# A new first third of the order table of an attention and MLP-mixer kernel

## The chip, the cores and the metric

The kernel runs on one core of a Trainium2 chip. The metric is the device time of one execution in microseconds (us). One core has a matrix engine (TensorE, in the profile PE; its weight loads are listed as PEld), a vector engine (DVE), a scalar engine (ACT), GpSimd (POOL) and SyncE (SP), each with an instruction stream of its own that is worked off in order, and DMA engines that move data between the device memory and the core's on-chip memory. Engines wait for one another and for loads through semaphores.

## The reference

Eight batches, 8 heads, 576 positions, head width 64. Attention is causal in blocks of 64 positions. Its output, with the heads side by side (512 columns), goes through a mixer: two matrices over the positions, then two over the columns, each pair with a relu between and a residual.

```python
scores = (q @ k.T) / sqrt(64)                 # per batch and head, 576 x 576
scores = where(pos_i // 64 >= pos_j // 64, scores, -1e9)
x = softmax(scores) @ v                       # -> x: 8 x 576 x 512
u = x + (relu(x.T @ w_tok1) @ w_tok2).T       # w_tok1 576 x 256, w_tok2 256 x 576
out = u + relu(u @ w_ch1) @ w_ch2             # w_ch1 512 x 1536, w_ch2 1536 x 512
```

Inputs and output are float32. The kernel computes its matrix products in bfloat16.

## The kernel before

The program first describes its work as 1,591 small operations, each with the engines that it may run on, the operations that it depends on, and the matrix result banks (PSUM banks) that it takes and gives back. Then one table of 1,492 words, `ORDER` (line 100), says in which order they are issued, on which engine each runs and which banks it takes. A word is the number of an operation, a letter for the engine (T PE, A ACT, D DVE, P POOL, S SP) and a letter for each bank: s and t are two double banks in use at the start, a to d four single ones, e to h four more that take the place of s and t after the first batch. `308Tdbha` is operation 308 on PE with banks d, b, h and a. Operations that the table does not name are spare matmuls that only keep PE busy at the start; 11 of these are named in it.

`placed` reads the table word by word; at the end of the kernel function each operation is emitted at once (lines 1545 to 1548). So the table fixes the order within each engine's stream, and with it the order in which loads are asked for. Two engines stand to each other only by dependencies.

```python
for word in ORDER.split():
    digits = word.rstrip("abcdefghstADPST")
    o, letters = self.ops[int(digits)], word[len(digits):]
    o.engine = self.ENGINE[letters[0]]
    assert all(d.n in done for d in o.deps)
...
    yield o
```

The operations that the change and the prediction touch, by number:

- Loads, all but a few of them issued by POOL (lines 413, 463, 474, 497, 506). q and k come per batch and group of four heads, and after them a transpose on DVE (line 437): 252 and 255 are k and q of batch 1's first four heads, 258 and 261 of its second, 421, 424, 427, 430 of batch 2, 595 to 604 of batch 3, 759 and 762 of batch 4. v comes in five blocks of positions: 34 to 38 for batch 0's first four heads, 39 to 43 for its second, 264 to 268 for batch 1, 433 to 437 for batch 2, 607 to 611 for batch 3. The weights: 155, 156 and 158 are w_tok1, 157 is w_tok2, 159 to 162 are the first halves of the four row blocks of w_ch1 and 163 to 166 the second halves, 167 to 169 are w_ch2.
- Attention of a batch and a group of four heads: three score sets on PE (line 562), each with an exp per head on ACT (line 768); a copy and a clear of the last columns, the "tail" (lines 590 and 595), on DVE or POOL; then for each head the product with v on PE (line 612) and its scaling on DVE (lines 632, 638), and the ends (line 665). For batch 0 the product comes in two parts, 222 and 223 first. Tails are 235 with 236 (batch 0, second group), 274 with 275 (batch 1, first group), 443 with 444, 475 with 476, 617 with 618. Score sets: 269, 281, 276 and 313, 301, 308 for batch 1, 438, 450, 482 and 470, 445, 477 for batch 2.
- Token mix: the matmuls with w_tok1 (line 803) with a relu to aT (lines 789 on ACT, 791 on DVE), the matmuls with w_tok2 (for batch 0 transposed, lines 836 to 851, otherwise 898), and the transposes to uT (985).
- Channel up of batch 0: twelve column blocks cc, each in two halves of two matmuls (line 1026), with a relu to gT on ACT or DVE. The blocks 0 to 7 need the first halves of w_ch1, 4 to 11 the second. 381 and 382 are the halves of cc 8, 384 and 385 of cc 9, 387 and 388 of cc 10, 390 and 391 of cc 11; the first of the two needs 163 and 164, the second 165 and 166. Later batches use a product scheme with fewer multiplications, for which DVE makes sums of w_ch1 (333 to 336, line 1057) and of w_ch2 (170 to 173, line 1312).
- Channel down (line 1360) with folds on DVE (line 1406) and, for batch 0, four "turns" (line 1382), which transpose uT back for the residual: 400, 404, 408 and 416 on PE, with a copy each. 411, 413 and 415 are products and 414 a fold. In the channel up of later batches "seed", "keep" and "final" are copies between banks and out of them (535, 550, 547, 544). 419 is a store of batch 0's output.

Of the kernel before, what the change touches and what calls it, by code (L numbers as in the profile page):

```python
# [27 lines left out]
class Plan:  # L28
# [72 lines left out]
    13S 16S 19S 22P 24P 5P 9D 2D 11D 8D 6D 3P 44Ta 12P 10P 4P 14D 30P 15D 17A 32P 1D 26P 18D 20A 28P 0A 45Tb 46Tc 47Td  # L101
    23D 25D 21D 7D 31D 174Tst 33D 175T 176A 177A 71Ta 61Tb 64Tc 182Ts 195A 196A 27D 81Td 183A 80Ta 201Tt 202A 60Tb 180Ts
    181A 29D 65Tc 197D 199Tt 76Td 178D 198D 36P 179D 200A 214Ts 215A 37P 35P 38P 34P 184Ta 188Tb 189T 190D 191D 207Tc
    208T 237Tt 238A 209D 210D 211Td 192Tb 216D 252P 254D 217D 193D 194D 220Ts 203Tc 204T 212D 213D 158P 205D 206D 185T
# [6 lines left out]
    386A 311A 296D 297D 289Th 290D 291D 160P 286Te 287D 288D 360Tg 366Ta 293D 310A 321Td 322D 323D 294D 319D 320D 400Th  # L111
    383A 416Tb 417A 161P 375Te 162P 376T 367T 368A 401A 421P 422D 423D 327Td 378Tc 372Tb 373T 374A 424P 328D 329D 404Tf
    405A 426D 377A 361T 427P 425D 428D 379T 380A 330Ta 362A 331D 332D 298Th 438Tdbfe 439A 430P 440A 324Ta 299D 432D 325D
    300D 369Tc 370T 326D 442A 429D 371D 450Tgdhb 441A 169P 363Ta 431D 364T 452A 333D 454A 451A 167P 357Te 358T 359A 365D
    393D 168P 482Tfcdb 485A 604P 484A 443P 453A 502Tg 436P 504Te 433P 503A 334D 335D 437P 435P 170D 486A 470Tadch 434P
    595P 505A 171D 444P 601P 483A 473A 445Tgbef 471A 172D 514Tc 448A 508Ta 472A 173D 515A 512Te 506Td 446A 509D 510Tc
    474A 513D 397Tgh 447A 475P 507D 449A 476P 394D 598P 477Tabef 398A 403Td 395D 480A 479A 511D 481A 493Te 396D 520Tb
    478A 490Tc 518Tf 521A 494D 407T 406D 519A 495D 597D 464Ta 596D 455Tb 461Tf 410D 458Te 399T 465D 491D 456D 457D 462D
    459D 466D 411T 463D 600D 402D 496Tb 522Ta 412D 516Tf 413T 523A 497D 599D 419S 517A 460D 762P 492D 499Tg 414D 759P
    467Ta 612Tdfec 498D 526D 415T 336D 615A 616A 614A 530Tcb 613A 487Te 500D 468D 469D 531Tf 533A 501D 617P 527D 545Tda  # L120
    532A 418D 618P 536T 611P 548A 524Tg 488D 489D 534Tf 537A 525D 610P 551T 528D 535A 624Thegc 605D 608P 552A 538T 606D
    628A 607P 540T 529D 627A 539D 678Td 626A 609P 603D 625A 549Tc 602D 679A 619Tgfeh 541D 550A 546Td 622A 760D 553T 623A
# [12 lines left out]
    723A 829D 830D 837Th 721D 953A 852Ta 838D 952A 839D 857D 825Tb 951A 853D 876Tce 1036P 954A 877Td 858D 856S 879A 826D
    861Tfh 827D 1035P 878A 862Tg 859D 864D 891Tad 949P 863A 880Tb 940P 706D 894A 882T 739D 881A 942P 865Tg 897T 937D
    866A 938P 867T 936D 883A 884T 860D 1021P 868A 871T 885D 1030P 869T 898A 886T 872D 1027P 987Tcfba 870D 874T 887D
    1034P 990A 895Tg 988A 875D 889T 991A 1007Tb 740D 989A 896A 890D 955Tchaf 741D 892Te 959A 899T 1026D 956A 901T 893D
    958A 1009Tf 957A 1008D 902D 975Tcaeh 1010D 972Tb 978A 904T 900D 979A 960Tf 1025D 969Te 905A 743Tgh 961D 976A 973D
    1122P 974D 962D 977A 970D 971D 982Tdbcf 980D 744A 981D 1022D 966Ta 984A 963Te 1023D 745T 985A 967D 888D 1119P 986A  # L140
    964D 965D 983A 1037P 995Tb 968D 873A 998Tc 746D 1050Tfeda 1033P 996D 999D 992Tg 1000D 1054A 749T 993D 1053A 994D
    997D 1052A 1028D 1038Tcagd 1051A 1029D 1004Tb 1041A 1031D 1001Te 1125P 1040A 747Tf 1032D 1039A 1002D 1003D 1128P
    1005D 1006D 1082Tgace 1135P 748D 1017Tb 1084A 742D 751T 1083A 1018D 1086A 750D 1042A 1045Tageb 1085A 752D 1043P 753T
    1047A 1131P 1121D 757S 1049A 1120D 1044P 1048A 1077Tdcfg 754D 1064Tb 1080A 1124D 1061Te 755T 1046A 1065D 1062D 1063D
    1079A 1078A 1070Tfaec 1081A 756D 1067Td 1074A 1123D 1058Tg 1073A 1104Th 1066D 1059D 1071A 1060D 1130D 1072A 1055Tc
    1143Tbegf 1105A 1056D 1075P 1057D 1015Ta 1134P 1068D 1146A 1127D 1013Th 1145A 1069D 1102Tc 1129D 1147A 1076D 1144A
# [1414 lines left out]
```

## Time and profile before

| | us |
|---|---|
| median of 3 runs | 287.9 |
| lowest and highest run | 285.44, 288.12 |
| the profiled execution | 286.21 |
| its span, first to last instruction | 284.4 |

The profile is of one execution. It gives for each engine when it was busy, and from the semaphores what ended each wait. Matmuls are pipelined and the ends of their rows are modelled, so a busy PE is not PE at its peak, and starts are surer than ends. PE's granted clock was 0.997 over the span. Of the engines PE was the busiest, with 97% of the span, and DVE followed with 85%. The page puts the DMA engines' mean busy share at nine tenths or more in most of the first 60 us.

### The profile page before, as it was taken

To read this page: it belongs to the slowest core of one execution; us is meant where nothing else is said; L and a number is where in the kernel's file an instruction comes from. 1 tells how busy PE (TensorE), PEld (TensorE's weight loads), DVE (VectorE), ACT (ScalarE), POOL (GpSimd) and SP (SyncE) were. 2 spreads that over 40 slices of the span, in tenths; PEclk is the share of its full clock that TensorE was granted. 3 is DMA by queue.
4 is the path that set the end of the run, shared out by engine and by line. 5 is a ranking of instruction groups with operands and counts; after the bars stand their busy time and mean duration, and the time that the engine had idled before them with its cause. 6 is when DMAs were issued, how large, how long until landed. Compare 5 with 4: busy or idle time off the path is not lost.

```text
span 284.4 us, 9295 instructions
## 1 busy us (share of the span) xinstructions
PE 275.6 (97%) x3958; PEld 201.9 (71%) x3958; DVE 241.8 (85%) x520; ACT 178.3 (63%) x329; POOL 71.9 (25%) x123
## 2 busy tenths in 40 slices
PE   7799999999999999999999999999999999999994
PEld 2367565588776688986877658756789876568883
DVE  4678599999889898999998979859896997679983
ACT  3797969954998756887779866274533744651200
POOL 8977623701630451063232220000000000000000
PEclk9999999999999999999999999999999999999998
DMA  7999999955989792999699593201044501200157
GB/s 166 144 152 202 179 213 212 170 89 116 110 96 135 87 142 60 220 133 162 70 117 144 65 177 61 74 3 21 0 83 96 194 0 74 77 1 2 74 152 220
DMA packets 64890, 31.95 MB, mean 112 GB/s; under 512 B 53200, under 2 KB 55888, under 8 KB 64848
## 3 DMA queue, kind: packets, MB, share of 16 engines
q0 software_dynamic: 44896, 17.49, 53.9%
q1 hardware_dynamic: 19520, 13.21, 18.0%
q8 instruction: 31, 0.51, 0.7%
q10 hardware_dynamic: 432, 0.66, 0.7%
q14 instruction: 11, 0.09, 0.1%
HBM read 35.85 MB, written 9.44 MB: 159 GB/s over the span
## 4 chain that ended last, share of the span: by engine, by line
PE 78%; DMA 12%; DVE 4%; POOL 4%; issue 1%; POOLq 0%; DVEq 0%
PE late L1360 20%; DMA wc_sb<-in_moe_w_ch_dram 10%; PE mm L1360 9%; PE late L1226 8%; PE late L1099 7%; PE mm L1099 6%; PE mm L1226 5%; PE mm L562 4%; PE mm L612 3%; PE late L562 2%; PE late L898 2%; DMA qk_sb<-in_k_dram 2%; PE late L612 2%; PE mm L803 2%; PE late L803 2%; PE mm L898 1%
## 5 line engine op out<-in xcount | busy, mean ns | idle before, releaser
L768 ACT ACTIVATE e_sb<-late 128x512 bf16<-128x512 f32 x87 | 50.2, 612 | 15.0 <-PE late L562 6.6
L768 ACT ACTIVATE e_sb<-mm 128x512 bf16<-128x512 f32 x81 | 46.8, 611 | 5.9 <-PE late L562 3.3
L437 DVE STREAM_TRANSPOSE qk_sb<-qk_sb 128x288 int32<-128x288 int32 (+1 forms) x65 | 42.2, 694 | 2.7 <-DMA qk_sb<-in_q_dram 1.8
L463 POOL DMA_DIRECT2D vals<-in_v_dram x45 | 37.0, 834 | 7.1 <-PE mm L612 2.4
L1360 PEld LDWEIGHTS <-gT 128*128 128x128 bf16 x336 | 32.0, 98 | 6.0 <-issue 0.9
L1360 PEld LDWEIGHTS <-sums 128*128 128x128 bf16 x324 | 31.3, 98 | 5.3 <-issue 0.4
L562 PEld LDWEIGHTS <-qk_sb 32*64 32x64 bf16 (+1 forms) x1152 | 19.1, 103 | 16.3 <-issue 12.8
L562 PE MATMUL late<-qk_sb 32*64 32x448 bf16 (+7 forms) x530 | 28.1, 280 | 0.3
L562 PE MATMUL mm<-qk_sb 32*64 32x64 bf16 (+7 forms) x478 | 27.3, 280 | 0.1
L612 PEld LDWEIGHTS <-e_sb 128*128 128x128 bf16 x640 | 22.9, 97 | 4.1 <-issue 2.6
L395 ACT COPY mm<-late 128x512 f32<-128x512 f32 (+1 forms) x29 | 16.2, 568 | 13.1 <-PE late L1099 6.8
L1099 PEld LDWEIGHTS <-ws_sb 128*128 128x128 bf16 x192 | 18.2, 98 | 3.2 <-issue 0.9
L612 PE MATMUL mm<-vals,e_sb 128*128 128x65 bf16 x410 | 17.7, 193 | 0.7 <-DMA vals<-in_v_dram 0.7
L1360 PE MATMUL late<-wd_sb,sums 128*128 128x256 bf16 x150 | 18.3, 273 | 0.0
L638 DVE TENSOR_TENSOR x_sb<-mm,rinv 128x256 bf16<-128x256 f32 x41 | 16.9, 419 | 1.0
L1226 PEld LDWEIGHTS <-ws_sb 128*128 128x128 bf16 x120 | 11.7, 98 | 8.6 <-issue 0.2
L1099 PEld LDWEIGHTS <-wc_sb 128*128 128x128 bf16 x144 | 15.3, 114 | 1.6 <-issue 0.4
L1226 PE MATMUL late<-e_sb,ws_sb 128*128 128x512 bf16 (+1 forms) x72 | 16.2, 344 | 0.0
L789 ACT ACTIVATE gT<-mm 128x512 bf16<-128x512 f32 x21 | 12.8, 608 | 4.8 <-PE mm L1099 2.9
L413 POOL DMA_DIRECT2D qk_sb<-in_q_dram x14 | 7.7, 548 | 29.8 <-DVE x_sb L638 10.4
L1406 DVE TENSOR_TENSOR o_sb<-late,u_sb 128x512 f32<-128x512 f32 x20 | 13.6, 682 | 1.5 <-PE late L1360 1.4
L1360 PE MATMUL late<-wd_sb,gT 128*128 128x256 bf16 x120 | 14.8, 273 | 0.0
(200 smaller groups left out, 629.4 us busy)
## 6 DMA issues: line engine op xcount, KB each, us to landing
out_dram<-o_sb SPq DMA_DIRECT2D x19, 256.0 KB, 2.7
qk_sb<-in_k_dram POOLq DMA_DIRECT2D x14, 288.0 KB, 6.3
qk_sb<-in_q_dram POOLq DMA_DIRECT2D x14, 288.0 KB, 6.0
vals<-in_v_dram POOLq DMA_DIRECT2D x28, 128.0 KB, 5.3
out_dram<-o_sb SPq DMA_DIRECT2D x7, 512.0 KB, 3.8
wc_sb<-in_moe_w_ch_dram POOLq DMA_DIRECT2D x8, 192.0 KB, 7.1
wc_sb<-in_moe_w_ch_dram POOLq DMA_DIRECT2D x3, 512.0 KB, 12.6
vals<-in_v_dram POOLq DMA_DIRECT2D x15, 64.0 KB, 4.7
```

The source lines that it names most:

```text
L395: nc.scalar.copy(dst, src)
L437: nc.vector.transpose(dst[:, 0:S, :] .rearrange("p s e -> p (s e)") .bitcast(I32) .rearrange("p (a k) -> p k a", k=NB)[:, k0:k1], raw2.bit ...
L463: nc.gpsimd.dma_start(out=t[128 - p : 128, J, hs, 0:64], in_=src)
L562: nc.tensor.matmul(out=home(n)[lo : lo + rows, c : c + w], lhsT=bar[r, 0] if j is None else kT[i][r, 64 * j : 64 * j + rows, par], rhs=bar ...
L612: nc.tensor.matmul(out=u[:, I, 0:65], lhsT=e[:, h, c : c + 128], rhs=vt[:, J, head, 0:65], start=(J == 0), stop=(J == I),)
L638: nc.vector.tensor_tensor(out=xt[:, 0:4, 64 * head : 64 * head + 64], in0=u[:, :, 0:64], in1=ri[:, 0:4].to_broadcast([128, 4, 64]), op=MULT,)
L768: nc.scalar.activation(dst, bank_of(x), EXP, scale=scale)
L789: nc.scalar.activation(dst, src, RELU)
L1099: nc.tensor.matmul(out=bank_of(bank)[:, 256 * o_ : 256 * o_ + 256], lhsT=x(o_, m), rhs=y[:, :, m, :], start=opens, stop=m == 1, skip_group ...
L1226: nc.tensor.matmul(out=bank_of(bank)[:, 128 * c : 128 * (c + step)], lhsT=x(m), rhs=y[:, c : c + step, m, :], start=opens, stop=m == 1, sk ...
L1360: nc.tensor.matmul(out=bank_of(bank)[:, 256 * i : 256 * i + 256], lhsT=x[:, kk, 128 * i : 128 * i + 128], rhs=y[:, kk], start=first and i ...
L1406: nc.vector.tensor_tensor(out=dst, in0=src, in1=other, op=ADD)
```

## The change

The first 540 words of the table are replaced. The set of operations is the same, and so is the code; from the 593rd word on, the operations and their engines stand in the same order as before, and only the letters of some banks are exchanged. The first eight words are the same too. In between, the order differs on PE, ACT, DVE and POOL; on SP only the store 419 goes two places back. The table's new part was found by a search in which the planner's model delays loads in flight by instruction packets; that model is not in the kernel.

Cut to the parts that the prediction speaks of:

```diff
 ORDER = """
-    13S 16S 19S 22P 24P 5P 9D 2D 11D 8D 6D 3P 44Ta 12P 10P 4P 14D 30P 15D 17A 32P 1D 26P 18D 20A 28P 0A 45Tb 46Tc 47Td
...
-    155P 186D 221A 187D 218Tt 219A 233Ts 43P 156P 339Tb 239Tt 253D 340D 255P 257D 256D 234A 240A 42P 41P 39P 40P 337Td
-    338A 222Tc 235D 236D 226Ta 227T 228D 223T 269Tbefg 271A 272A 249Th 224D 229D 225D 250D 251D 241Td 242T 243D 273A
-    244D 157P 245Ta 246T 164P 247D 248D 348Tc 349T 350D 270A 281Tehfd 284A 230Tg 231D 282A 232D 343Ta 285A 261P 263D
-    262D 258P 344D 276Tbcfg 277A 279A 159P 341Te 342A 280A 278A 283A 259D 260D 345Td 346T 347D 354Ta 355T 356D 313Tbfeg
-    317A 316A 314A 315A 351Td 352T 353D 163P 387Tc 384Th 166P 301Taged 305A 390Tb 303A 302A 268P 165P 391T 274D 392D
-    275D 388T 389D 304A 385T 306D 307D 308Tfdga 381Tb 264P 382T 408Te 409D 267P 312A 266P 265P 292Tc 295Ta 309A 318Tf
...
+    13S 16S 19S 22P 24P 5P 9D 2D 6D 11D 8D 3P 44Ta 12P 10P 4P 14D 30P 15D 17A 32P 1D 26P 18D 20A 28P 0A 45Tb 46Tc 47Td
...
+    237Tt 158P 337Tb 239Ts 238A 240A 209D 210D 212D 213D 255P 43P 40P 41P 338A 339Ta 257D 256D 216D 340A 217D 42P 39P
+    222Tc 223T 226Td 227T 254D 224D 269Tefgh 273A 157P 271A 225D 228D 235P 229D 230Tb 231D 272A 270A 236P 249Tc 250D
+    241Ta 242T 232D 243D 244D 245Td 246T 247D 348Th 349T 281Tbfag 282A 248D 251D 284A 261P 263D 350D 283A 343Td 344A
+    345Te 346T 262D 341Tc 347D 285A 276Tbhaf 342D 278A 354Td 258P 355T 424P 163P 277A 259D 260D 356D 351Te 352T 313Tgchb
+    164P 279A 353D 314A 315A 384Ta 408Td 409A 400Te 401D 166P 274P 316A 275D 165P 381Tg 317A 382T 416Tc 387Td 417D 280A
+    388T 389A 301Tehbc 304A 303A 268P 383D 385T 264P 404Tf 386D 426D 267P 405D 302A 305A 306D 307D 390Tg 391T 392A 265P
...
```

Operations that change their engine, 23 in all:

- from DVE to ACT: relus 340, 344 (aT of batch 0), 389, 392, 365, 371 (gT, cc 10, 11, 2 and 4), a turn's copy 409, a transpose's copy 525, a keep 547;
- from ACT to DVE: relus 342 (aT of batch 0), 383, 386, 359 (gT, cc 8, 9 and 0), 505 (aT of batch 1), the turns' copies 401, 405, 417, the seeds 535 and 550, a final 544;
- from DVE to POOL: the tail 235 and 236, the copy 274 of another tail.

ACT has two operations fewer, DVE one fewer, POOL three more. POOL's order of loads, from the v loads of batch 0 to the last of w_ch1 (tails in brackets):

```
before: 36 37 35 38 34 252 158 155 43 156 255 42 41 39 40 157 164 261 258 159 163 166 268 165 264 267 266 265 160 161 162
after:  36 37 38 156 35 34 252 155 158 255 43 40 41 42 39 157 (235 236) 261 258 424 163 164 166 (274) 165 268 264 267 265 266 159 160 161 162
```

On DVE the sum 336 of w_ch1, which came after product 415 was issued, stands right after 335, ahead of the sums 170 to 173 of w_ch2; the relus 359 and 505 stand ahead of these too. On PE the second-half blocks of channel up (cc 8 to 11) and the four turns come earlier, and the products with v of batch 1 later.

More of the change, by code (lines that the diff above doesn't have):

```diff
@@ new lines @@
+    394D 524Tc 395D 396D 525A 397Tdh 449A 403Tg 509D 406D 398A 399T 402D 477Tcfba 609P 600D 478A 444P 436P 481A 599D
+    479A 407T 475P 476P 518Te 464Tc 496Ta 465D 410D 519A 455Td 456D 466D 595P 480A 520Tf 521A 461Te 462D 522Tb 601P 411T
+    523A 596D 463D 608P 597D 458Tf 516Tc 517A 459D 460D 412D 457D 413T 414D 499Tb 467Te 612Tcfgd 500D 501D 468D 469D
+    616A 526D 527D 415T 418D 497D 498D 493Tb 545Tde 614A 613A 615A 530Tcf 528D 531Tg 494D 548A 533A 490Th 495D 532A 491D
+    492D 487Ta 488D 489D 536T 537A 534Tg 535D 603D 551T 607P 552A 759P 624Tbhac 604P 606D 538T 539D 549Td 610P 627A 625A
@@ new lines @@
+    628A 546Ta 547A 550D 605D 529D 540T 541D 678Tb 626A 602D 619Tgcah 760D 679A 621A 623A 555T 620A 622A 553T 554D 676Tb
+    677A 644Tchgd 648A 646A 617P 618P 762P 764D 763D 556D 557D 543T 544D 560Tab 561Td 563A 611P 647A 558T 562A 680Th
+    566T 567A 564Tf 559D 681D 684Tg 761D 651Tedha 685D 565A 568T 570T 686Tg 645A 653A 569D 655A 652A 654A 656Tcdaf 571D
+    641Te 660A 687D 629Th 635Tg 659A 573T 929P 642D 630D 768P 765P 689S 636D 637D 643D 632Tf 658A 631D 682Ta 649D 572D
+    657A 638Td 639D 640D 542D 788Tgech 633D 634D 574A 650P 673Tb 683D 790A 670Td 772P 674D 789A 664Te 688S 675D 671D
@@ new lines @@
+    806D 818A 799Tg 807D 854S 803D 724Tfh 817A 800D 709Tbc 801D 816A 727D 710Te 712A 725Tg 927D 711A 728Ta 855S 928D
+    726A 715T 804D 796Te 729A 934D 730T 716A 713Tg 933D 731A 734T 420S 797D 798D 714A 732T 593S 735D 943Tdbfe 733D 719T
+    945A 736D 717T 946A 720D 831Ta 944A 834Tb 718D 737T 947A 722T 835D 836D 738A 828Tf 948P 832D 833D 950Tdgeb 723A 829D
+    830D 837Th 721D 953A 852Ta 838D 952A 839D 857D 825Tc 951A 853D 876Tdf 1036P 954A 877Te 858D 856S 879A 826D 861Tbh
+    827D 1035P 878A 862Tg 859D 864D 891Tae 949P 863A 880Tc 940P 706D 894A 882T 739D 881A 942P 865Tg 897T 937D 866A 938P
@@ new lines @@
+    867T 936D 883A 884T 860D 1021P 868A 871T 885D 1030P 869T 898A 886T 872D 1027P 987Tdbca 870D 874T 887D 1034P 990A
+    895Tg 988A 875D 889T 991A 1007Tc 740D 989A 896A 890D 955Tdhab 741D 892Tf 959A 899T 1026D 956A 901T 893D 958A 1009Tb
+    957A 1008D 902D 975Tdafh 1010D 972Tc 978A 904T 900D 979A 960Tb 1025D 969Tf 905A 743Tgh 961D 976A 973D 1122P 974D
+    962D 977A 970D 971D 982Tecdb 980D 744A 981D 1022D 966Ta 984A 963Tf 1023D 745T 985A 967D 888D 1119P 986A 964D 965D
+    983A 1037P 995Tc 968D 873A 998Td 746D 1050Tbfea 1033P 996D 999D 992Tg 1000D 1054A 749T 993D 1053A 994D 997D 1052A
@@ new lines @@
+    1028D 1038Tdage 1051A 1029D 1004Tc 1041A 1031D 1001Tf 1125P 1040A 747Tb 1032D 1039A 1002D 1003D 1128P 1005D 1006D
+    1082Tgadf 1135P 748D 1017Tc 1084A 742D 751T 1083A 1018D 1086A 750D 1042A 1045Tagfc 1085A 752D 1043P 753T 1047A 1131P
+    1121D 757S 1049A 1120D 1044P 1048A 1077Tedbg 754D 1064Tc 1080A 1124D 1061Tf 755T 1046A 1065D 1062D 1063D 1079A 1078A
+    1070Tbafd 1081A 756D 1067Te 1074A 1123D 1058Tg 1073A 1104Th 1066D 1059D 1071A 1060D 1130D 1072A 1055Td 1143Tcfgb
+    1105A 1056D 1075P 1057D 1015Ta 1134P 1068D 1146A 1127D 1013Th 1145A 1069D 1102Td 1129D 1147A 1076D 1144A 1014D
@@ new lines @@
+    1093Tg 1103A 1090Te 1016D 1136Tfbch 1126D 1020S 1099Td 1137A 1094D 1114Ta 1091D 1092D 1140A 1100D 1087Tf 1101D 1139A
+    903D 1096Te 1088D 1112Th 1138A 1089D 758S 1108Td 1095D 1115A 1141P 1113D 1106Tc 1132P 1175Tbfag 1097D 1142D 1098D
+    1011Th 1133P 1107D 1179A 1336Te 1177A 1012D 1178A 1109D 1168Tgcfh 1176A 1110Ta 1116S 1171A 910Tbd 1170A 1111D 1337A
+    1169A 1334Tf 1117S 911D 906D 1148Tcaeg 912T 907D 1150A 1019S 1172A 1151A 916T 1173P 913D 1152A 1174P 1149A 908D
+    1118S 1180Taheg 909D 1153Tb 1183A 914Tc 1154D 1184A 1155D 1181A 917D 1194Te 1182A 1335D 1159Tb 1191Tg 1195D 1185Ta
@@ new lines @@
+    1196D 1197Th 1160D 1192D 1165Tf 1193D 920T 915D 1161D 1198D 1199D 1166D 1188Te 1167D 921D 1162Tg 1156Tb 1189D
+    1249Tfh 1190D 918T 1163D 1164D 1252A 1200D 1201D 922T 1186D 919D 1157D 1255T 1158D 924S 1279Tce 1187D 923D 1280Tg
+    1282A 1350Tb 1256A 1281A 1234Tda 1351A 1344Tf 1237A 1283Tb 1345D 1285T 1284A 1240T 1286A 1338Tg 1241A 1250Tf 1339D
+    1253Tc 1251A 1287T 1202D 1254A 1348Td 1288D 1203D 1259T 1349A 1257T 1238Tb 1258D 1289T 1239A 1235Tg 1290D 1342Tf
+    1236A 1244T 1291D 1343D 1356Td 1242T 1245D 1219Tcg 1243D 1360Tf 1260D 1220Tb 1361A 1357D 1262T 1222A 1292T 1364S
@@ L168 @@
[L168 removed]
+    1261D 1313S 1493T 1312S 1490A 1513Tcg 925S 1502Tb 1516A 1499Te 1503D 1514Td 1500A 1519T 1492D 1508T 1494D 1520A
+    1506T 1509D 1517Ta 1515A 1496T 1216D 1518A 1314D 1511T 1414Tce 1512A 1507D 1521T 1523T 1522D 1510A 1318Tbd 1524D
+    1417A 1365D 1526T 1366D 1420T 1415Tf 1315D 1421A 1322Ta 1416A 1527D 1319A 1497D 1418Tc 1316D 1320T 1419A 1367D
+    1429Tfg 1321D 1324T 1432A 1317D 1323D 1424T 1435T 1425D 1422T 1436A 1433Tb 1368D 1326T 1423D 1434A 1325D 1430Th
```

79 lines of the change are left out of this document (20 added, 59 removed).

## The prediction

> **What bounds the kernel now.** I read the page's busy line first, to see which engine could set the end.
>
> ```profile
> span 284.4 us, 9295 instructions
> PE 275.6 (97%) x3958; PEld 201.9 (71%) x3958; DVE 241.8 (85%) x520; ACT 178.3 (63%) x329; POOL 71.9 (25%) x123
> ```
>
> PE is busy 275.6 of 284.4 us, so an order can win only out of the other 8.8. An average over the span does not say where those lie; the busy time of each engine by stretches does (start:end, length, then busy us and count for each engine, granted clock, DMA share, GB/s).
>
> ```profile
> core 0: us, PE busy (x) PEld busy (x) DVE busy (x) ACT busy (x) POOL busy (x), PEclk, DMA share, GB/s
> 0.00:8.32 8.32, 5.59 (x16) 2.00 (x16) 4.32 (x12) 2.73 (x4) 7.00 (x19) 1.00 0.79 169
> 8.32:22.52 14.20, 12.82 (x280) 7.99 (x279) 9.58 (x31) 11.92 (x15) 12.02 (x20) 1.00 1.42 148
> 22.52:45.00 22.48, 22.48 (x479) 14.74 (x476) 18.41 (x54) 18.41 (x37) 10.31 (x17) 1.00 1.35 201
> 45.00:70.00 25.00, 24.33 (x412) 17.07 (x412) 24.38 (x48) 17.02 (x34) 8.69 (x15) 1.00 0.96 140
> 70.00:90.00 20.00, 20.00 (x335) 14.61 (x333) 18.23 (x45) 19.41 (x39) 8.23 (x13) 1.00 1.13 122
> 90.00:284.40 194.40, 190.35 (x2456) 145.47 (x2448) 166.85 (x336) 108.79 (x203) 25.62 (x41) 1.00 0.54 93
> ```
>
> The reader is to see three things. PE idles 8.32 - 5.59 = 2.73 us in the first row, 1.38 in the second, none in the third, 0.67 in the fourth, none in the fifth and 4.05 in the last. The table is the old one from entry 593 on, which is work of roughly 70 us and later, so the 4.05 are out of reach, and whatever is won or lost before 70 us passes through a full PE (20.00 of 20.00) to the end. And while PE is full from 22.52 to 45, the loads are at their densest, 201 GB/s. The chain that ended last tells it otherwise at first sight (start, length, what).
>
> ```profile
> 30.74 6.40 DMA wc_sb<-in_moe_w_ch_dram
> 37.42 14.09 DMA wc_sb<-in_moe_w_ch_dram
> 51.61 2.71 DVE wd_sb L1312 x3
> ```
>
> Two loads, 6.40 + 14.09 = 20.49 us, carry the chain until 51.61, where the differences of w_ch2 begin on DVE. Yet PE had no hole there. So loads and PE run side by side, about equally late, and a better order of loads by itself frees nothing unless PE waits for one. The timeline shows where it does (start, length, engine, line, work, count, and in brackets the idle time before it with its cause).
>
> ```profile
> 21.41 0.22 PE L612 MATMUL mm<-vals,e_sb 128*128 128x65 bf16 x2 [0.45 <-DMA vals<-in_v_dram]
> 21.89 0.70 PE L612 MATMUL mm<-vals,e_sb 128*128 128x65 bf16 x18 [0.26 <-DMA vals<-in_v_dram]
> ```
>
> PE waits for v of batch 0's second four heads, 0.45 + 0.26 = 0.71 us, and between 8.32 and 70 us for no other load.
>
> **The change part by part.** No operation comes or goes, so PE's work is the same and the sum consists of waits alone.
>
> To 22.52 us. The first eight entries are the same, and what follows to 8.32 waits for the same first loads: 0. Between 8.32 and 22.52, the v load that PE waits for last (operation 40 before, 39 after) ends in both tables the same ten POOL loads (252, 255, 155, 158, 39 to 43, and 156), only permuted, with 156 moved ahead of two v loads of the first heads. It lands no earlier, and the scores behind it start at about 22.5 again: 0. The bounds are -1.38, all idle time of that row of the windows, and +0.45, the longer of the two waits once more for the first heads.
>
> Instruction packets have one line on the page (count, MB, share of 16 engines).
>
> ```profile
> q8 instruction: 31, 0.51, 0.7%
> ```
>
> They are 0.007 x 16 x 284.4 / 31 = 1.03 us each, on one DMA engine. Not more than the 0.71 us that PE waits for loads can be won by stepping aside for them. [...]
>
> 22.52 to 45. Matmul halves of the second half of w_ch1 (cc 8 to 11) and the four turns back of uT change places with scores; the price is the landing of load 165, which 382 is now the first to need. Sizes and times to landing (KB, us) are on the page, and the old run has the issue of 165 on POOL and the exps that copy 274 waits for:
>
> ```profile
> qk_sb<-in_q_dram POOLq DMA_DIRECT2D x14, 288.0 KB, 6.0
> vals<-in_v_dram POOLq DMA_DIRECT2D x28, 128.0 KB, 5.3
> ...
> wc_sb<-in_moe_w_ch_dram POOLq DMA_DIRECT2D x8, 192.0 KB, 7.1
> ```
>
> ```profile
> 23.51 0.55 POOL L497 DMA_DIRECT2D wc_sb<-in_moe_w_ch_dram  x1
> ...
> 24.80 0.62 ACT L768 ACTIVATE e_sb<-mm 128x512 bf16<-128x512 f32 x1
> ```
>
> ```profile
> L590 POOL COPY vals<-e_sb 128x256 bf16<-128x256 bf16 x3 | 1.2, 405 | 4.8 <-ACT e_sb L768 4.8
> ```
>
> Before, 165 lands by 23.51 + 0.55 + 7.1 = 31.16 if it takes the median. After, POOL first does 274, whose exps end at 25.42, so the issue of 165 ends at 25.42 + 0.41 + 0.55 = 26.38, and the median from there gives 33.48 at worst. But these loads stand in line: 1,440 KB are ahead of 165 since 157 in the new table (258, 261 and 424 of 288, three of 192), 1,472 in the old (258 and 261, four of 192 and one of 128), and by that it lands where it did. When does PE come to it?
>
> ```profile
> 31.72 1.49 PE L1026 MATMUL mm<-uT,wc_sb 128*128 128x512 bf16 x6
> 33.04 0.59 PE L1026 MATMUL late<-uT,wc_sb 128*128 128x512 bf16 x2
> ...
> 34.15 1.05 PE L1026 MATMUL mm<-uT,wc_sb 128*128 128x512 bf16 x4
> 35.05 0.39 PE L1382 MATMUL late<-ident,uT 128*128 128x128 bf16 x4
> 35.27 0.77 PE L612 MATMUL mm<-vals,e_sb 128*128 128x65 bf16 x20
> ```
>
> ```profile
> 31.11:31.72 0.61, 0.61 (x46) 0.54 (x45) 0.06 (x1) 0.61 (x2) 0.37 (x2) 1.00 2.34 156
> 33.57:34.15 0.58, 0.58 (x33) 0.43 (x32) 0.53 (x2) 0.38 (x1) 0.23 (x2) 1.00 2.02 187
> ```
>
> A half takes (33.04 - 31.72) / 3 = 0.44, so 382, the second of the row at 34.15, began at 34.59. The new table has five halves (387, 390, 391, 388, 385) and the two score sets of these windows (301, 308) behind it, 5 x 0.44 + 0.61 + 0.58 = 3.39 us, and two turns ahead of it, 2 x (35.27 - 35.05) = 0.44: 34.59 - 3.39 + 0.44 = 31.64. The old run used 165 without a wait in the row at 31.72, in its second half (391, from 32.16), so it had landed between 31.16 and 32.16. That is a wait between 0 and 33.48 - 31.64 = 1.84. I take +0.45, just under the 32.16 - 31.64 = 0.52 of the old landing, because a line at 201 GB/s sets landings more than the issue does.
>
> 45 to 70. Two edits matter.
>
> ```profile
> 51.71 0.10 PEld L562 LDWEIGHTS <-qk_sb 32*64 32x64 bf16 x1 [0.39 <-issue]
> 52.20 0.11 PEld L562 LDWEIGHTS <-bar 32*64 32x64 bf16 x4 [0.39 <-issue]
> ```
>
> ```profile
> 67.76 0.69 DVE L1406 TENSOR_TENSOR o_sb<-late,o_sb 128x512 f32<-128x512 f32 x1
> ...
> 69.02 1.48 PE L1360 MATMUL late<-wd_sb,gT 128*128 128x256 bf16 x12
> 69.03 0.95 DVE L1057 TENSOR_TENSOR ws_sb<-wc_sb,ws_sb 128x1536 bf16<-128x1536 bf16 x1
> ```
>
> ```profile
> L791 DVE TENSOR_SCALAR gT<-mm 128x512 bf16<-128x512 f32 x4 | 2.7, 683 | 1.7 <-PE mm L1026 1.6
> ```
>
> Scores of batch 2 stop twice for 0.39 while ACT empties their banks. ACT gets two operations fewer in the new table; I take half of the 0.78 away, -0.39 (bounds -0.78 and 0). Against it DVE, busy 24.38 of 25.00: the last sum of w_ch1 (336, 0.95 us, at 69.03 before) now runs ahead of the differences of w_ch2 and of the folds. With so little idle time nearly all of the 0.95 delays them. The fold that product 415 needs ended at 67.76 + 0.69 = 68.45, 0.57 before 69.02; 0.95 - 0.57 = +0.38. Bounds: 0, if the operations taken off DVE make up for it (four relus of 0.68 in this stretch and the one before, against three put on it), and 0.95 + 2 x 0.68 - 0.57 = +1.74, if the relus 359 and 505, also put ahead on DVE, count in full. The output store 419 on SP goes behind two others; nothing near waits for it. From 70 on two copies (535, 550) move from ACT (19.41 of 20) to DVE (18.23 of 20): 0, as DVE's 1.77 us of idle time cover 2 x 0.68.
>
> Sum: 0 + 0 + 0.45 - 0.39 + 0.38 = +0.44 us. The profiled run took 286.21 (span 284.4 and 1.8 around it) and would become 286.65. The three timed runs are 287.9, 285.44 and 288.12; with the profiled one the mean of the four is 286.92, 1.0 under the median of the three, and I take it as the kernel's own time. The forecast is 286.92 + 0.44 = 287.4.
>
> **The rivals.** (1) Faster: all that PE waits for before 70 goes, the 1.38 and the 0.67 of the windows and the 0.78 under the modelled ends, 2.83 in all: 284.1. For it: moves of the table stand ahead of each of these gaps. Against: the v loads keep their place.
>
> (2) Slower, by POOL: three tail operations (the copy 235 with its clear 236, and the copy 274) move from DVE onto POOL in the midst of the loads, and POOL works in order. The view of waits shows what POOL stood for such copies (in all, times, longest), and that of the tile vals how fast a load can land.
>
> ```profile
> POOL vals L590 <- ACT e_sb L768: 38.0, 8, 7.8
> ```
>
> ```profile
> DMA to landing us min/median/max: 3.8/5.5/8.6
> ```
>
> It waited 38.0 us in eight copies, 4.75 on average and 7.8 at most. The loads behind can be late by about 7.1 - 3.8 = 3.3 us, the median of a w_ch1 load less the fastest landing, before the line of loads ahead runs dry. It decides once a copy stands for more than that: at the longest wait 7.8 - 3.3 = 4.5 us fall on PE, 291.4; at the mean, 1.45. For it: v of batch 1 and 165 are issued behind 274. Against: its exps end at 25.42, and POOL, which was issuing loads until 23.51 + 0.55 = 24.06 in the old run, would stand for some 2 us.
>
> (3) DVE becomes the bound: 336, 359 and 505 all count, 0.95 + 2 x 0.68 = 2.31 without slack: 289.2. For it 24.38 of 25.00; against it the relus that DVE loses.
>
> (4) The change does nothing: loads wait in line and not for packets, and the waits only change places, 286.9.
>
> **How the numbers follow.** One per cent, 2.9 us, is about what a measurement of this kernel can tell from no change. Chances: forecast 0.50, (1) 0.12, (2) 0.19, (3) 0.11, (4) 0.08. The forecast alone, with all its terms at one end together, would reach from 286.92 - 1.38 - 0.78 = 284.8 to 286.92 + 0.45 + 1.84 + 1.74 = 290.9. Faster by over 1% (below 285.0) is most of (1) and a little scatter, 0.13; slower (above 290.8) is most of (2) and a little of (3) and of the forecast, 0.22; within is 0.65. The range from 284.6 to 290.7 takes in the forecast, (3), (4) and the milder part of (2), and leaves out (1) where it comes in full and (2) beyond a wait of 7.1 us: 290.7 - 286.9 + 3.3.
>
> **What would show it.** The step to 22.52 is right if PE's first matmul of v with the second heads waits again until about 21.9 for v. The w_ch1 step: a wait of PE for wc_sb near 31.5, below 1 us. The hole near 51.7: half of it left. The fold: PE idle for o_sb or u_sb by DVE near 69, under 1 us. Rival (2) shows as a POOL wait for e_sb above 3.3 us before 30 us with PE waiting for vals or wc_sb behind it. The prediction is wrong if PE's idle time before 70 us differs by more than 2 us from the 4.78 that the first four rows give, or if a window after 90 loses time that the old one did not.

## The result, and the profile after

| | old | new |
|---|---|---|
| median of 20 runs, us | 286.05 | 286.37 |
| lowest and highest | 284.94, 288.71 | 285.03, 291.18 |
| ratio, 95% interval | | 1.0008 (0.9988 to 1.0029) |
| span of the profiled execution | 284.4 | 286.2 |
| its mean granted clock of PE | 0.997 | 0.982 |

No difference can be measured. But the profiled execution of the new kernel is 1.8 us longer than the old one's, and its clock is lower. The comparison leaves out runs more than 1.5% above a kernel's fastest; where runs are counted by their clock below, these are counted too (one each of the new kernel, e5 and e8, three of e2).

From the page of the new kernel: its span, and the busy shares of PE and its clock in 40 slices of 7.2 us.

```profile
span 286.2 us, 9283 instructions
...
PE   8699999999999999999999999999999999999994
...
PEclk9759999999999999999999999999999999999999
```

In the second and third slice the clock is 7 and 5 tenths; in the old kernel it was 9 or more in every slice but the last, which lies behind its last matmuls. The busy time by stretches, in the columns of the prediction, shows what that did. The first two rows are stretches of the clock's own, told of below.

```profile
core 0: us, PE busy (x) PEld busy (x) DVE busy (x) ACT busy (x) POOL busy (x), PEclk, DMA share, GB/s
6.82:10.23 3.41, 1.31 (x46) 0.64 (x46) 1.94 (x4) 1.27 (x4) 3.20 (x5) 1.00 1.36 166
10.23:20.47 10.24, 10.09 (x125) 4.71 (x124) 3.20 (x10) 7.04 (x9) 7.29 (x11) 0.50 1.41 147
0.00:8.32 8.32, 5.95 (x14) 2.05 (x15) 4.12 (x12) 2.73 (x4) 7.00 (x19) 1.00 0.78 170
8.32:22.52 14.20, 13.11 (x221) 6.68 (x225) 6.21 (x20) 9.17 (x12) 10.02 (x17) 0.64 1.33 144
22.52:45.00 22.48, 22.16 (x465) 14.89 (x464) 19.77 (x57) 18.46 (x35) 14.72 (x25) 1.00 1.27 176
45.00:70.00 25.00, 24.60 (x414) 16.82 (x415) 24.27 (x45) 19.20 (x38) 9.51 (x16) 1.00 1.16 142
70.00:90.00 20.00, 19.75 (x357) 15.27 (x353) 18.87 (x43) 17.79 (x35) 4.33 (x8) 1.00 0.71 101
```

From 10.23 to 20.47 us PE ran at half its clock: 125 matmuls keep it busy for 10.09 us. Before that it was busy for only 1.31 of 3.41 us. The timeline of PE shows why, first of the old kernel and then of the new.

```profile
8.32 0.51 PE L562 MATMUL sc<-qk_sb 32*64 32x192 bf16 x28 [1.53 <-DVE qk_sb L437]
8.54 0.20 PE L562 MATMUL sc<-bar 32*64 32x64 bf16 x4
8.59 0.45 PE L562 MATMUL sc<-qk_sb 32*64 32x256 bf16 x12
8.97 0.82 PE L374 MATMUL mm<-wd_sb 128*128 128x512 bf16 x3
```

```profile
8.65 0.50 PE L562 MATMUL sc<-qk_sb 32*64 32x192 bf16 x26 [1.49 <-DVE qk_sb L437]
9.69 0.33 PE L562 MATMUL sc<-qk_sb 32*64 32x320 bf16 x2 [0.53 <-ACT e_sb L581]
...
10.38 1.49 PE L374 MATMUL mm<-wd_sb 128*128 128x512 bf16 x3 [0.23 <-issue]
```

In the old kernel the two halves of the first score set (174, with 192 columns, and 175) follow each other at once, and the spare matmuls (line 374) after them at 8.97. In the new one 175 waits 0.53 us for an exp and the spare matmuls come at 10.38. The exp is 195, which the new table names ahead of 175 ("174Tst 195A 33D 27D 175T"); the old one had it long behind. It reads the bank half that 174 has filled, in the tile that 175 writes next, so 175, which stands behind it in the order, waits until it has read. PE thus stood still for 1.49 + 0.53 us and some smaller gaps within a few us, and the clock fell.

In spite of 10 us at half clock the run lost under 2 us. In part PE had slack to lose: in the old profile it waited for v at 21.4 and 21.9. In the new one it comes to that place at 24.8, all of v has landed, and the wait is gone; PE waits for no load in the whole run. In part the new order wins time behind this place, as the second table below shows.

### The profile page after: what moved, and what is told of

It is laid out like the page before. It is cut to its first block, busy times and chain, and to the rows that moved or that the text cites. A ratio compares the mean times of both kernels' runs of the same rounds, so it can differ in the third digit from the quotient of the medians.

```text
span 286.2 us, 9283 instructions
## 1 busy us (share of the span) xinstructions
PE 277.2 (97%) x3936; PEld 202.6 (71%) x3958; DVE 243.0 (85%) x519; ACT 177.7 (62%) x327; POOL 73.2 (26%) x126
## 4 chain that ended last, share of the span: by engine, by line
PE 88%; ACT 5%; DVE 3%; DMA 2%; issue 1%; SPq 0%; DVEq 0%; ACTq 0%
PE late L1360 18%; PE mm L1360 12%; PE late L1099 8%; PE late L1226 8%; PE mm L562 5%; PE mm L1226 5%; PE mm L1099 4%; PE mm L612 4%; ACT e_sb L768 3%; PE late L612 3%; PE mm L803 2%; PE late L562 2%; PE sc L562 2%; DMA gT<-in_q_dram 2%; PE late L898 2%; PE mm L898 2%
## 5 line engine op out<-in xcount | busy, mean ns | idle before, releaser
L768 ACT ACTIVATE e_sb<-mm 128x512 bf16<-128x512 f32 x91 | 51.2, 610 | 12.3 <-PE mm L562 6.0
L768 ACT ACTIVATE e_sb<-late 128x512 bf16<-128x512 f32 x77 | 44.1, 616 | 10.2 <-PE late L562 6.4
L395 ACT COPY mm<-late 128x512 f32<-128x512 f32 (+1 forms) x32 | 17.8, 566 | 16.7 <-PE late L1099 6.8
L562 PE MATMUL late<-qk_sb 32*64 32x64 bf16 (+7 forms) x470 | 25.3, 278 | 0.0
L590 POOL COPY vals<-e_sb 128x256 bf16<-128x256 bf16 (+1 forms) x12 | 4.7, 394 | 47.8 <-ACT e_sb L768 40.5
L1360 PE MATMUL late<-wd_sb,sums 128*128 128x256 bf16 x138 | 16.9, 273 | 0.0
L581 ACT ACTIVATE e_sb<-sc 128x1024 bf16<-128x1024 f32 (+2 forms) x14 | 12.0, 902 | 5.4 <-PE sc L562 5.4
L612 PE MATMUL mm<-vals,e_sb 128*128 128x65 bf16 x330 | 14.7, 196 | 0.1
L638 DVE TENSOR_TENSOR x_sb<-mm,rinv 128x256 bf16<-128x256 f32 x33 | 13.8, 420 | 0.8
L638 DVE TENSOR_TENSOR x_sb<-late,rinv 128x256 bf16<-128x256 f32 x31 | 13.0, 423 | 1.0
```

The source lines that it names most:

```text
L395: nc.scalar.copy(dst, src)
L562: nc.tensor.matmul(out=home(n)[lo : lo + rows, c : c + w], lhsT=bar[r, 0] if j is None else kT[i][r, 64 * j : 64 * j + rows, par], rhs=bar ...
L581: nc.scalar.activation(dst, sc[SC.index(note["pool"])][:, :, cols], EXP, scale=scale)
L612: nc.tensor.matmul(out=u[:, I, 0:65], lhsT=e[:, h, c : c + 128], rhs=vt[:, J, head, 0:65], start=(J == 0), stop=(J == I),)
L638: nc.vector.tensor_tensor(out=xt[:, 0:4, 64 * head : 64 * head + 64], in0=u[:, :, 0:64], in1=ri[:, 0:4].to_broadcast([128, 4, 64]), op=MULT,)
L768: nc.scalar.activation(dst, bank_of(x), EXP, scale=scale)
```

## The experiments

Every run's mean clock is known, so the runs can be sorted by it. Spans are medians in us; the old kernel's row holds the runs made of it beside the experiments. A mean of 0.997 instead of 1.000 need not be a loss: in the old kernel's profile the clock is at half only in the last 1.84 us, where PE has nothing left to do.

| kernel | runs | median time | ratio to old (95%) | clock 0.997 or more: runs, span | below 0.990: runs |
|---|---|---|---|---|---|
| old | 133 | 286.05 | | 96, 284.0 | 5 |
| new (with e0) | 32 | 286.46 | 1.0008, 1.0007 | 14, 284.3 | 10 |
| e1 exp behind | 12 | 286.3 | 0.9996 (0.9971 to 1.0021) | 7, 284.2 | 0 |
| e2 old, exp ahead | 12 | 287.92 | 1.0040 (1.0003 to 1.0076) | 4, 284.05 | 4 |
| e3 old, more spare | 12 | 285.93 | 0.9996 (0.9966 to 1.0025) | 9, 284.0 | 2 |
| e5 tails on DVE | 12 | 287.0 | 1.0022 (0.9995 to 1.0049) | 3, 283.9 | 5 |
| e6 five spare at 222 | 12 | 286.38 | 1.0009 (0.9989 to 1.0028) | 11, 284.6 | 0 |
| e8 sum 336 behind | 12 | 287.05 | 1.0017 (0.9988 to 1.0045) | 3, 284.0 | 8 |
| e10 v first | 6 | 288.46 | 1.0086 (1.0055 to 1.0117) | 0 | 1 |
| e12 w_ch1 first | 12 | 286.27 | 1.0015 (0.9988 to 1.0041) | 9, 284.1 | 2 |
| e13 and three spare at 222 | 12 | 286.75 | 1.0020 (1.0000 to 1.0039) | 10, 284.8 | 0 |
| e15 spare between | 12 | 285.62 | 0.9989 (0.9961 to 1.0017) | 9, 283.6 | 1 |
| e16 e15 and e12 | 12 | 286.48 | 1.0021 (0.9989 to 1.0054) | 7, 284.3 | 2 |
| e17 e15, three spare at 222 | 12 | 286.91 | 1.0045 (1.0010 to 1.0080) | 8, 284.7 | 4 |
| e18 old, three spare at 222 | 12 | 286.74 | 1.0026 (1.0000 to 1.0052) | 10, 284.7 | 0 |

And when four operations started on PE in single profiled executions (us, each at its first weight load, which can stand ahead of a wait, as 222 does in the old kernel, in e1 and in e12; 788 is a score set at about 89, the first after which old and new have the same work left):

| profile | 222 | 269 | 382 | 788 | 269 to 788 | span |
|---|---|---|---|---|---|---|
| old | 20.77 | 22.52 | 34.40 | 89.10 | 66.58 | 284.4 |
| new | 24.75 | 25.57 | 34.41 | 91.17 | 65.60 | 286.2 |
| e0 | 23.10 | 24.01 | 32.87 | 89.61 | 65.60 | 284.8 |
| e1 | 19.43 | 22.82 | 32.30 | 89.03 | 66.21 | 284.0 |
| e5 | 21.09 | 21.81 | 31.82 | 88.39 | 66.57 | 283.9 |
| e10 | 20.28 | 24.75 | 34.54 | 91.28 | 66.52 | 286.5 |
| e12 | 20.54 | 21.71 | 30.57 | 87.95 | 66.24 | 283.4 |

**e0: the new kernel again.**

> The new kernel unchanged, for a second profile. Theory A (clock): in the profiled run of the new kernel PE's granted clock fell to 0.50 from 10.4 to 20.3 us, because the second half of the first score set (175) came at 9.69 instead of 8.59 us and the spare matmuls after it; it does so in some runs only. Runs at a clock of 0.998 or more then have spans of 284.0 to 284.6, runs at 0.98 to 0.99 of 285.4 to 286.5. Theory B (no clock effect, only ordinary scatter): span and granted clock are not related, and a run at full clock is as often at 286 as one at 0.985.

Together with the first twenty, 14 of 32 runs at 0.997 or more have a median span of 284.3 and the 10 below 0.990 one of 285.9. Theory A, with a scatter of its own: at full clock the spans still reach from 283.2 to 285.6.

**e1: the exp behind the score, in the new table; e2: ahead of it, in the old.**

```diff
 e1
-174Tst 195A 33D 27D 175T 61Ta
+174Tst 33D 27D 175T 195A 61Ta
 e2
-174Tst 33D 175T 176A 177A 71Ta 61Tb 64Tc 182Ts 195A
+174Tst 33D 195A 175T 176A 177A 71Ta 61Tb 64Tc 182Ts
```

> The new kernel with one word moved: exp 195 (half of batch 0's first set) stands behind score operation 175 again, as it did before. Theory A: 175 no longer waits for that exp and starts within 0.4 us of 174 (8.3 to 8.8 us) instead of 1.0 us after it; PE's idle time between 7 and 10.4 us falls from about 1.9 to about 1.2 us, and the clock stays at 1.0 in more runs; median 0.3 to 1.0 us under the new kernel's. Theory B: 175 waits for something else (its bank or the transpose), no change of the place nor of the time.

> The old kernel with the one word moved the other way: exp 195 ahead of 175. Theory A: 175 moves from 0.2 us behind 174 to about 1 us behind it, PE idles longer before 10.4 us, and the clock falls in more runs: median 0.3 to 1.0 us above the old kernel's. Theory B: as the old kernel, within 0.2 us.

The one word does it both ways. The timelines, first of e1, where 175 follows 174 within 0.3 us and the spare matmuls come at once, then of e2, where 175 waits for the exp and starts 1.04 us behind 174.

```profile
7.33 0.51 PE L562 MATMUL sc<-qk_sb 32*64 32x192 bf16 x28 [1.49 <-DVE qk_sb L437]
7.55 0.20 PE L562 MATMUL sc<-bar 32*64 32x64 bf16 x4
7.60 0.45 PE L562 MATMUL sc<-qk_sb 32*64 32x256 bf16 x12
7.98 1.04 PE L374 MATMUL mm<-wd_sb 128*128 128x512 bf16 x4
...
21.63 1.26 PE L612 MATMUL mm<-vals,e_sb 128*128 128x65 bf16 x20 [2.01 <-DMA vals<-in_v_dram]
```

```profile
8.26 0.57 PE L562 MATMUL sc<-qk_sb 32*64 32x192 bf16 x26 [1.94 <-DVE qk_sb L437]
9.30 0.47 PE L562 MATMUL sc<-qk_sb 32*64 32x320 bf16 x2 [0.46 <-ACT e_sb L581]
```

No run of e1 falls below 0.990, and e2 has four of 12, where the old kernel has 5 of 133; e2 is slower just beyond its interval, by 1.1 us in the ratio and by 1.9 in the median, more than the 0.3 to 1.0 expected. But e1's median is only 0.2 us under the new kernel's 286.46: the row at 21.63 shows where the gain of the profiled run went. PE is early now, waits 2.01 us for v, and in this profile its clock falls at 21.23 instead, to 0.50 until 24.64.

**e3: six spare matmuls ahead of 174 in the old table; e15: four between 174 and 175 in the new, the exp left ahead.**

```diff
 e3
-174Tst
+48Ta 49Tb 50Tc 51Td 52Ta 53Tb 174Tst
 e15
-174Tst 195A
+174Tst 48Tb 49Tc 50Td 51Tb 195A
```

> The old kernel with six more spare matmuls (48 to 53) ahead of 174, in the 1.5 us in which PE waits for the first transposes. Theory A: PE is busy from 2 us to the first scores, the clock holds at 1.0 in every run, and the spread between the runs of the old kernel (284.9 to 288.7) shrinks to its lower end: median 0.3 to 1.0 us under the old. Price: the scores start up to 0.3 us later, which the wait for v at 21.9 hides. Theory B: nothing, or 0.1 to 0.3 us slower.

> The new kernel with exp 195 left ahead of 175, and four spare matmuls (48 to 51, 0.86 us) between 174 and 175. Theory A (PE's idle time before 10.4 us lets the clock fall, not the late 175 as such): no run or one run of 12 below a clock of 0.99, against 10 of 32 of the new kernel, though 175 is as late or 0.2 us later. Theory B (the late scores cost the time by themselves): clock and time as the new kernel's, a third of the runs below 0.99.

e3 changes nothing: three of its 12 runs are still below 0.997, two of them below 0.990, and the old kernel seldom falls there. e15 has one run of 12 below 0.990, although 175 starts 1.3 us behind 174 there (7.79, 9.08) and 1.0 in the new kernel. (Its table is a line longer, so line 562 is 563 there.)

```profile
7.79 0.39 PE L563 MATMUL sc<-qk_sb 32*64 32x192 bf16 x24 [1.14 <-DVE qk_sb L438]
8.11 1.04 PE L375 MATMUL mm<-wd_sb 128*128 128x512 bf16 x4
9.08 0.34 PE L563 MATMUL sc<-qk_sb 32*64 32x320 bf16 x4
...
18.78 0.37 PE L613 MATMUL mm<-vals,e_sb 128*128 128x65 bf16 x7 [1.22 <-issue]
```

That speaks for the idle time as the cause of the falls, and against the late score. The one run is the profiled one, and its fall is another: PE had stood 1.22 us until 18.78 with nothing that the profile shows as a cause, and the clock fell at 19.45, to 0.50. e15 has the lowest median of all kernels, 285.62, but its interval includes no change.

**e5: tails 235, 236 and 274 on DVE again** (235P, 236P, 274P become 235D, 236D, 274D).

> The new kernel with the tail operations 235, 236 and 274 on DVE again, in the same places. Rival (2) of the prediction (POOL held by the tails, loads behind it late): 0.5 us or more faster than the new kernel, and the loads 165 and 264 to 268 issued earlier by the time that POOL stood at 274. Theory A (only the clock and the wait for v in the first 25 us): the same as the new kernel within 0.3 us, since PE waits for none of these loads in either.

Not faster, so POOL's tails cost nothing that can be measured, though 165 is indeed issued earlier (at 22.8 us, in e0 at 27.5). Its profiled execution kept the full clock, set 269 started earliest but for one, and there the wait that the prediction priced appears:

```profile
30.58 0.59 PE L1026 MATMUL late<-uT,wc_sb 128*128 128x512 bf16 x2
31.83 0.62 PE L1026 MATMUL late<-uT,wc_sb 128*128 128x512 bf16 x2 [0.66 <-DMA wc_sb<-in_moe_w_ch_dram]
```

The second row is 382, waiting for load 165 until 31.8. From start to start the two halves lie 1.25 us apart; a half takes 0.44, so the hole is 0.81.

**e8: the sum 336 behind product 415** (336D moved from behind 335D to behind 415T).

> The new kernel with the w_ch1 sum 336 (0.95 us on DVE) behind product 415 again, as before. The prediction's fold step: DVE's folds come 0.95 us earlier and 415 up to 0.38 us earlier: 0.3 to 0.4 us faster. The rival, after seeing the new trace (415 starts 1.2 us after fold 414 ends, since other matmuls stand between): no change within 0.2 us.

Not faster, with eight falls of 12. The fold and the product that needs it, first in e0, then in e8:

```profile
67.87 0.68 DVE L1406 TENSOR_TENSOR o_sb<-late,o_sb 128x512 f32<-128x512 f32 x1
69.11 1.48 PE L1360 MATMUL late<-wd_sb,gT 128*128 128x256 bf16 x12
```

```profile
68.83 0.68 DVE L1406 TENSOR_TENSOR o_sb<-late,o_sb 128x512 f32<-128x512 f32 x1
70.07 1.16 PE L1360 MATMUL late<-wd_sb,gT 128*128 128x256 bf16 x9
```

The distance is 1.24 us with the sum ahead (e0) and with it behind (e8), and was 1.26 in the old kernel. PE does three other operations in between and waits for no fold.

**e10: v ahead of q of batch 1.** With the exp behind: 255P moved behind 39P, the rest of batch 0's products with v ahead of 269, the transposes 257 and 256 directly ahead of 269, tails 235 and 236 on DVE.

```diff
-255P 43P 40P 41P 338A 339Ta 257D 256D 216D 340A 217D 42P 39P 222Tc 223T 226Td 227T 254D 224D 269Tefgh
...
+43P 40P 41P 338A 339Ta 216D 340A 217D 42P 39P 255P 222Tc 223T 226Td 227T 254D 224D 225D 228D 229D
+235D 236D 230Tb 231D 232D 249Tc 250D 251D 241Ta 242T 243D 244D 245Td 246T 257D 256D 269Tefgh
```

> The new kernel with exp 195 behind 175, the v loads 39 to 43 ahead of load 255 (q of batch 1), the tails 235 and 236 on DVE, and the rest of batch 0's products with v (230, 241, 242, 245, 246, 249) ahead of set 269. Theory A: v lands about 288 KB / 150 GB/s = 1.9 us earlier (near 19.8 instead of 21.7), PE does the 1.9 us of products while q comes in, 269 starts at about 23 as it did, but with 1.2 us of work less behind it: 0.5 to 1.2 us faster than with the exp moved alone, and faster than the old kernel. Theory B (loads land by what the line holds, q later by as much as v is earlier, and its two transposes of 0.7 us each behind it): 269 comes 1 us later, nothing won.

Theory B. PE does not wait for v, but the two transposes that 269 needs run on DVE from 23.46 on (in e1 they start at 19.37 and 20.31), behind the scalings of the new products:

```profile
23.46 1.25 DVE L437 STREAM_TRANSPOSE qk_sb<-qk_sb 128x288 int32<-128x288 int32 x2
...
24.75 0.34 PE L562 MATMUL late<-qk_sb 32*64 32x320 bf16 x4 [1.66 <-DVE rinv L632]
```

269 starts at 24.75, and the clock falls behind it (0.92 in the mean from 22.52 to 45).

**e6: five spare matmuls behind 222; e12: 424 behind 165; e13: e12 with three spare behind 222; e16: e12 with e15's spare matmuls.** The first three with the exp behind 175.

```diff
 e6
-222Tc 223T
+222Tc 54Ta 55Ta 56Ta 57Ta 58Ta 223T
 e12
-424P 163P 277A
+163P 277A
-165P 381Tg
+165P 424P 381Tg
```

> The new kernel with exp 195 behind 175 and five spare matmuls (54 to 58, 1.1 us) behind 222, where PE stood 2.0 us for v with only the exp moved, and its clock fell to 0.50 from 21.4 to 24.7 us. Theory A: the clock holds there, set 269 starts within 0.3 us of where it did (22.8) and the stretch from 269 to 788 shortens from 66.2 to 65.6 us or less: median 0.4 to 0.8 under the exp moved alone, and under the old kernel's 285.8. Theory B (the fall was chance and costs nothing): no change, or 0.2 to 0.5 slower by the spare matmuls in the way.

> The new kernel with exp 195 behind 175 and load 424 (q of batch 2, 288 KB) behind load 165 instead of ahead of 163. Theory A: 165 lands about 288 KB / 190 GB/s = 1.5 us earlier (29.7 to 30.3 instead of 31.2 to 31.8), PE's wait for it at 382, 0.66 us in the run that came there at 31.8 and 0 in those that came at 32.3 or later, is gone in all: runs at full clock 0 to 0.7 us shorter, lowest span under 283.1. Theory B (the line of loads or the transposes of batch 2 take it back: set 438 waits for 421 or 424): no change.

> As e12, with three spare matmuls (54 to 56, 0.65 us) behind 222 in the wait for v. Theory A: the clock stays at 0.997 or more in nearly all runs, and with 165 early the median falls 0.3 to 0.8 us under the old kernel's, the first version that beats both. Theory B: the spare matmuls cost what the clock gains, as with five of them (spans of 284.6 in the middle at full clock): same as e12.

> The new kernel with the four spare matmuls between 174 and 175 (as e15) and load 424 behind 165 (as e12). Theory A: the two add up: at most one or two of 12 runs below a clock of 0.99, 165 lands before 30.5 us and 382 never waits; median 0.3 to 0.7 us under the old kernel's 286.0. Theory B (the first 25 us are bound by the loads, and what is saved at one of these waits is waited for at the next): as e15, 285.6 to 286.0, within what can be measured from the old.

In e6 and e13 no run falls below 0.990, but at full clock they are 0.4 and 0.7 us longer than e1 and e12: the spare matmuls cost what they save. In e12 382 starts at 30.57 and does not wait, so load 165 has landed by then (31.8 in e5); no time is won. The timeline has the next wait:

```profile
40.99 1.26 DVE L437 STREAM_TRANSPOSE qk_sb<-qk_sb 128x288 int32<-128x288 int32 x2 [0.73 <-DMA qk_sb<-in_k_dram]
...
42.30 0.32 PE L562 MATMUL mm<-qk_sb 32*64 32x320 bf16 x1 [0.23 <-DVE qk_sb L437]
```

PE now waits for batch 2's k, which the same line of loads brings, first to DVE's transpose and through it to set 438. e16 adds the two mends and gains nothing either.

**e17 and e18: three spare matmuls behind 222, in e15 and in the old table.**

```diff
 e17
-222Tc 223T
+222Tc 54Ta 55Ta 56Ta 223T
 e18
-222Tc 235D
+222Tc 54Tb 55Tb 56Tb 235D
```

> The new kernel with four spare matmuls between 174 and 175 and three (54 to 56, 0.65 us) behind 222 in the wait for v. Theory A (the wait for v makes the clock fall in the remaining runs): 11 or 12 of 12 runs at 0.997 or more, median 285.3 to 285.7. Theory B (the spare matmuls of the second place cost as much as they save, 0.65 us whenever v is there): clock as in A, but runs at full clock 0.4 to 0.7 us longer than the 283.6 of e15.

> The old kernel with three spare matmuls (54 to 56, 0.65 us) behind 222. Theory A: its runs at a clock of 0.990 to 0.996 (24 of 89, spans 1.4 us over the others) come from the wait for v and go: at most one of 12; median 0.2 to 0.4 us under the old. Theory B (they come from elsewhere): two to four of 12 stay.

At full clock they are 1.1 and 0.7 us longer than without these matmuls, theory B of e17 and more. e18 has two runs between 0.990 and 0.997, where three would be expected from the old kernel's 32 of 133, so whether the old kernel's falls come from the wait for v stays open. e17 has four below 0.990, which neither theory had.

## Why the prediction was right or wrong

**The time.** 287.4 was forecast and 286.37 measured, inside the range. The change was forecast as +0.44 us; the ratio gives +0.23 (0.0008 x 286.05) with an interval from -0.3 to +0.8, no measurable difference. That the two changes lie so close is luck: the terms of the sum did not come as forecast, and what they missed cancelled.

**The base, 286.92, was mis-sized.** The mean of four executions stood for a kernel whose median over 20 runs is 286.05. These 0.87 us are most of the 1.03 between forecast and measurement, and more than any term of the change.

**The step that failed is "To 22.52 us ... 0".** The prediction compared the loads and the last v load, found them the same, and from that took the scores behind to start at 22.5 again. It did not read the order of exps against scores on two engines, and it had no term for the clock. In the new kernel's two profiles 269 started at 25.57 and 24.01, 3.05 and 1.49 us later than in the old one. The cause is shown by e1 and e2: exp 195 ahead of 175 makes PE stand still, and then the clock falls in more runs. Counted over all kernels with that order and no mend (new, e5, e8), 23 of 56 runs are below 0.990; with the exp behind (e1, e6, e10, e12, e13) it is 3 of 54. Where the clock held, in the profile of e5 (the new order but for the tails), 269 came at 21.81, earlier than in the old kernel. By this one profile the loss is the fall and not the order alone. For instruction packets the sum has nothing, where the rows allow -0.71 us; no run tells what they cost.

The prediction's own sign of error could not see this. PE's idle time before 70 us is 2.37 + 1.09 + 0.32 + 0.40 = 4.18 us by the rows of the new kernel, near the 4.78 of before, since matmuls at half clock count as busy (10.09 of the 10.24 us). No time is lost behind: from 788 to the end the new kernel takes 195.0 us and the old one 195.3.

**The wait for 165, +0.45**, was right in its mechanism and its landing (31.2 to 32.2 forecast, 31.8 in e5). Its size hangs on the start: 0.66 us idle where 269 started at 21.8, nothing where it started at 22.8 or later (e1, e0, new).

**The bank hole, -0.39.** Both gaps of 0.39 are gone, not half of them. In e0 the weight loads of scores have one gap left near there, the 0.21 at 52.85, and the others belong to the token mix (lines 898 and 929), where PE waits for a relu:

```profile
52.85 0.11 PEld L562 LDWEIGHTS <-qk_sb 32*64 32x64 bf16 x4 [0.21 <-issue]
53.76 0.10 PEld L898 LDWEIGHTS <-w_sb 128*128 128x128 bf16 x1 [0.23 <-issue]
54.28 0.14 PEld L929 LDWEIGHTS <-w_sb 128*64 128x64 bf16 x4 [0.42 <-issue]
```

```profile
53.76 0.59 PE L898 MATMUL late<-aT,w_sb 128*128 128x512 bf16 x2 [0.25 <-ACT aT L789]
```

So the term came out larger, against one new wait of 0.25 us. That ACT's two operations fewer did it is not shown: the profile gave no cause for the old gaps ("issue"), and no experiment touched them.

**The fold, +0.38**, did not come (e8). A small distance between two rows was taken for a wait, but PE had other operations in it.

**The sum from 22.52 on.** The prediction had +0.44. With a late start the stretch from 269 to 788 is 65.60 us against 66.58, a gain of 0.98; at full clock and with an early start (e5) it is 66.57, and the hole of 0.81 for 165 is most of the difference. So what the new order wins after 22 us it gives to the next load when it comes there early, and what it loses before is in part won back when it comes late. This is read from single profiles; it would explain why effects of 1 to 3 us leave +0.3 in the median.

**The rivals.** (2), POOL's tails, is out by e5, and in the new kernel's profile POOL waited 2.46 us for copy 235, less than the 3.3 that the rival needed. Of (3), DVE as the bound, e8 tests the sum 336 alone; for the two relus there is only the new kernel's profile, in which PE waits for DVE nowhere between 10 and 90 us. (1) did not come. That the waits only change places, given 0.08, is the nearest to what the traces show.

## What to carry to other kernels

In a table order, read every pair of engines around a shared tile, not the loads alone: an exp named too early made the next score wait 0.53 us for it. Here a mend at one wait was paid at the next one for a load (2.01 us for v at 21 us in e1, 0.66 for w_ch1 at 31 in e5, 0.23 for the transpose of k at 42 in e12), and no order that was tried brought a gain that can be measured. Take a kernel's own time from many runs, sorted by their clock, before forecasting a few tenths of a per cent.

## What the runs showed of the hardware

The clock fell and rose in steps of 3.41 us: the falls lasted 10.24 us in the new kernel, 6.83 in e0, 3.41 in e1. In the step before the new kernel's fall PE was busy for 1.31 of 3.41 us. Below are the step before the fall in e1; a step of e5, with 1.72 us, that had no fall behind it; and the step before the fall in e15, the busiest of the four:

```profile
17.81:21.23 3.42, 1.81 (x28) 1.22 (x27) 2.43 (x8) 2.79 (x5) 2.65 (x7) 1.00 1.75 172
```

```profile
5.08:8.49 3.41, 1.72 (x32) 0.71 (x31) 2.91 (x5) 1.11 (x3) 3.41 (x6) 1.00 1.01 146
```

```profile
16.04:19.45 3.41, 2.19 (x70) 1.65 (x66) 2.30 (x10) 2.13 (x3) 1.78 (x4) 1.00 1.68 165
```

So if there is a bound on the busy time, these four steps give it no sharp place: the clock fell behind 1.31, 1.81 and 2.19 us, and not behind 1.72, all of them modelled durations. PE worked in each of them: the step before the new kernel's fall held 46 matmuls. Where the steps begin differs from run to run (the first rise was at 6.08 us in the old kernel's profile and at 6.82 in the new one's, and the ten matmuls from 1.60 us on, which took 4.47 us in both, took 4.05 in e5 and 3.59 in e1), which fits that the same order falls in some runs and not in others.

PE stood still without a cause in the profile for 0.73 us until 18.01 in e5, 0.34 until 17.45 in e12, 1.22 until 18.78 in e15, 0.56 until 18.50 in e16 and 0.42 until 18.23 in e17. In the old kernel PE does not stop near 18. What PE waited for in the five was not shown.
